# A weight load in two parts, parity copies, and another exit in a depthwise-separable kernel

## Chip, cores, metric

One core of one Trainium2 chip. The metric is the device time of one execution in microseconds (us), the median of several runs. The kernel before took 575.16 us (575.14 to 575.4, 3 runs). The engines are TensorE (PE; its weight loads are PEld), VectorE (DVE), ScalarE (ACT), GpSimd (POOL) and SyncE (SP).

## The reference, cut to what matters

```python
x:  (1, 384, 384, 384) bf16      # 147456 rows of 384 channels, 113 MB
dw: (1, 1, 384)                  # a 1x1 depthwise filter: one factor per channel
pw: (384, 384)
out = einsum('bhwc,cd->bhwd', x * dw, pw)
```

With a 1x1 filter this is one matrix product: x times a 384 x 384 matrix whose row c is dw[c] * pw[c].

## The kernel before

The rows are worked in 288 blocks of 512. VectorE transposes 32 x 32 squares of 32-bit words (channel pairs), so that channel pairs come to lie on the 32 partitions of a square. TensorE then runs 48 matmuls a block, four at a time, each on its own 32 rows of the array. ScalarE moves each finished block out of PSUM, and SyncE stores it.

Since TensorE works on four row groups, each needs its own copy of the scaled weights, split by even and odd channel. That makes six 128 x 768 pieces of `w_r`, made at the start by matmuls with a selector matrix `sel_w` that already holds dw:

```python
nc.scalar.dma_start(dw_row[:], ...).then_inc(s_dw, 16)
load_x(0, nc.scalar)                                           # x0
nc.sync.dma_start(pw_n[:], pw.rearrange("(k p) d -> p k d", p=P)).then_inc(s_pw, 16)
...                                                            # x1, x2, ... on SyncE
idle_work(4)                                # TensorE: 4 rounds of 4 matmuls on ones
nc.tensor.wait_ge(s_dw, 16)
for k in range(3): ...                      # dw onto partitions, by three matmuls
idle_work(4)
nc.tensor.wait_ge(s_pw, 16)
times = {(1, 1): 3, (2, 0): 2}              # some products are repeated
for k in range(3):
    nc.tensor.wait_ge(s_sw, k + 1)          # selector k is ready (VectorE)
    for r in range(2):
        if k == 2:
            nc.tensor.wait_ge(*w_done[r])   # copy r has left PSUM
        for v in [0, 1] * times.get((k, r), 1):
            mm = nc.tensor.matmul(PS[(k + 1) % 2][:, 2 * r + v, :D],
                lhsT=sel_w[64 * v : 64 * v + 64, k, r, :, :]...,
                rhs=pw_n[64 * v : 64 * v + 64, k, :], ..., tile_position=(64 * v, 0))
        mm.then_inc(s_w)                    # then a copy on ScalarE or VectorE into w_r
```

The main loop follows; its first step waits for four of the six copies. At the end:

```python
nc.sync.wait_ge(s_a[je % 2], je // 2 + 2 + k)     # ScalarE's half of the last block
nc.sync.wait_ge(s_d, k + 1)                       # VectorE's half
nc.sync.dma_start(dst[:, part], src[:, part]).then_inc(s_o[g % NR], 16)
```

## Time and profile before

| | kernel before |
|---|---|
| median time | 575.16 us |
| profiled span | 573.2 us |
| first main matmul | 6.90 us |
| block spacing | 1.950 us, all 287 steps |
| last block's copies begin, to the end | 4.47 us |

Shares of busy time say little here: TensorE is busy 99% of the span by design, also with idle matmuls. The useful views are the chain of waits, which says what held the start of the loop, and the timeline of the two ends. The prediction below shows and reads those lines. One line of that timeline: start us, us, engine, line, operation, tiles, count, and the idle time before it with its releaser.

```profile
5.49 0.66 PE L239 MATMUL ps<-pw_n,sel_w 64*128 64x384 bf16 x6 [0.17 <-ACT w_r L289]
```

Six matmuls take 0.66 us, because they run two at a time on the two halves of the array's rows.

### The profile page before, as it was taken

Reading aid. Unit: us, or ns where it says so; the run is one execution under the profiler, and the core shown is the slowest. Engines: PE = TensorE matmul, PEld = TensorE weight load, DVE = VectorE, ACT = ScalarE, POOL = GpSimd, SP = SyncE. Lnnn points to the kernel's source line nnn. Section 1 sums busy time; section 2 is a strip of 40 time slices with the busy share of each in tenths; the row PEclk is TensorE's granted clock in tenths of the full one; section 3 lists DMA queues with packets and bytes.
Section 4 is the critical chain, followed back from the end, with each engine's and each line's share of the span. In section 5 each row is a group of like instructions: output and inputs, shape, how many; then the busy total and the mean of one; then the engine's idle time right before and its main releaser. Section 6 shows DMA issues by size and latency. Waiting matters only on the chain.

```text
span 573.2 us, 29721 instructions
## 1 busy us (share of the span) xinstructions
PE 566.5 (99%) x13877; PEld 417.7 (73%) x13877; DVE 509.0 (89%) x584; ACT 418.7 (73%) x297; POOL 0.5 (0%) x5
## 2 busy tenths in 40 slices
PE   8999999999999999999999999999999999999996
PEld 5777777777777777777777777777777777777774
DVE  7899999999999999999999999999999999999995
ACT  6777777777777777777777777777777777777775
POOL 0000000000000000000000000000000000000000
PEclk9999999999999999999999999999999999999999
DMA  8999999999999999999999999999999999998676
GB/s 361 427 334 432 422 424 433 443 413 424 430 420 411 391 396 433 399 387 401 425 400 389 406 423 400 399 394 423 411 387 428 403 391 406 413 398 365 265 288 238
DMA packets 26452, 226.88 MB, mean 396 GB/s; under 512 B 1225, under 2 KB 6986, under 8 KB 22602
## 3 DMA queue, kind: packets, MB, share of 16 engines
q1 hardware_dynamic: 25264, 225.61, 97.1%
q10 hardware_dynamic: 1178, 1.18, 0.6%
q14 instruction: 9, 0.07, 0.0%
q8 instruction: 1, 0.02, 0.0%
HBM read 113.54 MB, written 113.25 MB: 396 GB/s over the span
## 4 chain that ended last, share of the span: by engine, by line
PE 97%; DMA 1%; ACT 1%; DVE 0%; issue 0%; SPq 0%
PE ps L191 97%; DMA pw_n<-in_pw_dram 1%; DMA out_dram<-O 0%; ACT w_r L289 0%; ACT O L326 0%; DVE O L324 0%; PE ps L239 0%; SPq L359 0%; SPq L102 0%
## 5 line engine op out<-in xcount | busy, mean ns | idle before, releaser
L191 PE MATMUL ps<-w_r,T 32*128 32x384 bf16 x13824 | 561.8, 321 | 0.7 <-ACT w_r L289 0.7
L276 DVE STREAM_TRANSPOSE T<-X 128x384 uint32<-128x384 uint32 x572 | 502.2, 880 | 53.9 <-DMA X<-in_x_dram 0.4
L191 PEld LDWEIGHTS ps<-w_r,T 32*128 32x128 bf16 x13824 | 415.9, 93 | 146.6 <-issue 1.0
L326 ACT CAST O<-ps 128x1536 bf16<-128x1536 f32 x287 | 412.7, 1438 | 147.3 <-PE ps L191 147.3
L289 ACT CAST w_r<-ps 128x768 bf16<-128x768 f32 x5 | 3.6, 820 | 1.0 <-PE ps L239 1.0
L208 PE MATMUL ps<-const-bfloat16-1.0 32*128 32x384 bf16 x32 | 2.9, 515 | 1.1 <-SPq L102 1.1
L276 DVE STREAM_TRANSPOSE T<-Xl 128x384 uint32<-128x384 uint32 x4 | 3.5, 880 | 0.4
L324 DVE CAST O<-ps 128x384 bf16<-128x384 f32 x2 | 1.0, 553 | 3.1 <-DMA out_dram<-O 3.1
L264 ACT ACT_TABLE_LOAD x1 | 1.3, 1283 | 1.9 <-issue 1.9
L208 PEld LDWEIGHTS ps<-const-bfloat16-1.0 32*128 32x128 bf16 x32 | 1.1, 125 | 1.7 <-issue 1.4
L239 PE MATMUL ps<-pw_n,sel_w 64*128 64x384 bf16 x18 | 1.8, 324 | 0.3 <-ACT w_r L289 0.2
L239 PEld LDWEIGHTS ps<-pw_n,sel_w 64*128 64x128 bf16 x18 | 0.7, 94 | 1.8 <-DMA pw_n<-in_pw_dram 0.9
L289 DVE CAST w_r<-ps 128x768 bf16<-128x768 f32 x1 | 1.0, 957 | 0.9 <-PE ps L239 0.9
L294 DVE TENSOR_REDUCE sel<-eye 128x64 f32<-128x128 bf16 x1 | 0.3, 290 | 1.4 <-POOL eye L254 1.4
L323 ACT CAST O<-ps 128x384 bf16<-128x384 f32 x2 | 0.9, 482 | 0.5 <-PE ps L191 0.5
L301 DVE COPY dw_f<-ps 128x3 f32<-128x3 f32 x1 | 0.2, 161 | 1.0 <-PE ps L221 1.0
L304 DVE TENSOR_SCALAR sel_w<-sel,dw_f 128x256 bf16<-128x256 f32 x3 | 0.9, 348 | 0.0
L221 PEld LDWEIGHTS ps<-const-bfloat16-1.0,dw_row 1*128 1x128 bf16 x3 | 0.2, 102 | 0.6 <-DMA dw_row<-in_dw_dram 0.6
L264 ACT COPY warm<-const-float32-0.0 128x1 f32<-128x1 f32 x2 | 0.3, 190 | 0.0
L254 POOL TENSOR_SCALAR_AFFINE_SELECT eye<-const-bfloat16-1.0 128x128 bf16<-128x128 bf16 x1 | 0.3, 292 | 0.6 <-SPq L102 0.6
L221 PE MATMUL ps<-const-bfloat16-1.0,dw_row 1*128 1x1 bf16 x3 | 0.2, 167 | 0.0
L348 POOL MEMSET const-bfloat16-1.0<- 128x1 bf16 x1 | 0.1, 102 | 0.0
(3 smaller groups left out, 0.3 us busy)
## 6 DMA issues: line engine op xcount, KB each, us to landing
X<-in_x_dram SPq DMA_DIRECT2D x26, 3840.0 KB, 21.2
out_dram<-O SPq DMA_DIRECT2D x26, 3840.0 KB, 27.1
X<-in_x_dram SPq DMA_DIRECT2D x3, 1536.0 KB, 17.4
out_dram<-O SPq DMA_DIRECT2D x4, 768.0 KB, 9.2
out_dram<-O SPq DMA_DIRECT2D x2, 1536.0 KB, 14.7
X<-in_x_dram SPq DMA_DIRECT2D x3, 768.0 KB, 7.4
X<-in_x_dram SPq DMA_DIRECT2D x1, 2304.0 KB, 19.1
out_dram<-O SPq DMA_DIRECT2D x1, 2304.0 KB, 10.9
```

What stands on the lines that cost most here:

```text
L191: mm = nc.tensor.matmul(PS[s][:, q, :D], lhsT=Ts[s][32 * q : 32 * q + 32, b, par::2], rhs=w_r[32 * q : 32 * q + 32, b, par, :], start=(b, ...
L208: nc.tensor.matmul(PS[0][:, 2 * (i % 2) + i // 2, :D], lhsT=ones[32 * i : 32 * i + 32, 0:P], rhs=ones[32 * i : 32 * i + 32, :], start=True ...
L221: mm = nc.tensor.matmul(PS[1][:, 0, D + k : D + k + 1], lhsT=dw_row[:, P * k : P * k + P], rhs=ones[0:1, 0:1], start=True, stop=True,)
L239: mm = nc.tensor.matmul(PS[(k + 1) % 2][:, 2 * r + v, :D], lhsT=sel_w[64 * v : 64 * v + 64, k, r, :, :].rearrange("p q w -> p (q w)"), rhs ...
L254: nc.gpsimd.affine_select(out=eye[:], in_=ones[:, 0:P], pattern=[[-1, P]], compare_op=mybir.AluOpType.is_equal, fill=0.0, base=0, channel_ ...
L264: nc.scalar.copy(warm[:, s : s + 1], nc.const_aps.tensor(0.0, [P, 1], F32)).then_inc(s_a[s])
L276: ins = nc.vector.transpose(out=Tw[:, 3 * h : 3 * h + 3], in_=Xw[:, :, j, 96 * h : 96 * h + 96].rearrange("p k (b w) -> p b k w", w=32),)
L289: o = nc.vector.tensor_copy(out, in_) if e == 0 else nc.scalar.copy(out, in_)
L304: nc.vector.tensor_scalar_mul(sel_w[:, k], sel[:].unsqueeze(2).to_broadcast([P, 2, 4, 32]), dw_f[:, k : k + 1]).then_inc(s_sw)
L323: nc.scalar.copy(Ov[:, q, j, :], PS[s][:, q, :D]).then_inc(s_a[s])
L324: nc.vector.tensor_copy(Ov[:, q + 1, j, :], PS[s][:, q + 1, :D]).then_inc(s_d)
L326: a = nc.scalar.copy(Ov[:, :, j, :], PS[s][:, :, :D])
```

## The change

The intent: get the first part of pw sooner and in longer runs, so that the weight copies and the loop start sooner, and shorten the tail. Rows 0 to 255 of pw go two per partition (1536 bytes in one run), then x0, then rows 256 to 383 onto 64 partitions, all on SyncE's queue. Since neighbouring rows now share a partition, the products are split by row parity. The critical section is opened and closed by GpSimd, and SyncE's two last waits change places.

```diff
-    with tc.tile_critical():
+    with tc.tile_critical(sync_engine=mybir.EngineType.Pool, no_gpsimd_drain=True):
...
+                nc.sync.wait_ge(s_d, k + 1)
                 nc.sync.wait_ge(s_a[je % 2], je // 2 + 2 + k)
-                nc.sync.wait_ge(s_d, k + 1)
...
-        load_x(0, nc.scalar)
-        nc.sync.dma_start(pw_n[:], pw.rearrange("(k p) d -> p k d", p=P)).then_inc(s_pw, 16)
+        nc.sync.dma_start(
+            pw_n[:, 0:2].rearrange("p t d -> p (t d)"),
+            pw[0 : 2 * P, :].rearrange("(p t) d -> p (t d)", t=2),
+        ).then_inc(s_pw, 16)
+        load_x(0)
+        nc.sync.dma_start(
+            pw_n[0:64, 2:4].rearrange("p t d -> p (t d)"),
+            pw[2 * P : C, :].rearrange("(p t) d -> p (t d)", t=2),
+        ).then_inc(s_pw2, 16)
...
-        for k in range(3):
+        for k in range(4):
+            c0, m = (k, P) if k < 2 else (2 * P + k - 2, 64)
             mm = nc.tensor.matmul(
-                PS[1][:, 0, D + k : D + k + 1],
-                lhsT=dw_row[:, P * k : P * k + P],
+                PS[1][0:m, 0, D + k : D + k + 1],
+                lhsT=dw_row[:, c0 : c0 + 2 * m - 1 : 2],
...
+                tile_position=(0, 0),
...
                 for v in [0, 1] * times.get((k, r), 1):
+                    row, slot, h = (64 * v, r, k) if k < 2 else (0, 2 + r, v)
...
-                        tile_position=(64 * v, 0),
+                        tile_position=(row, 0),
```

Left out: the waits that go with it, four selectors instead of three, another order of two steps within a block, and the places in `w_r` that the copies write.

More of the change, by code (lines that the diff above doesn't have):

```diff
@@ L67 @@
     psum = ctx.enter_context(tc.tile_pool(name="psum", bufs=1, space=bass.MemoryType.PSUM))
-    pw_n = consts.tile([P, 3, D], BF16, name="pw_n")
+    pw_n = consts.tile([P, 4, D], BF16, name="pw_n")
     eye = consts.tile([P, P], BF16, name="eye")
     sel = consts.tile([P, 2, 32], F32, name="sel")
-    sel_w = consts.tile([P, 3, 2, 4, 32], BF16, name="sel_w")
+    sel_w = consts.tile([P, 4, 2, 4, 32], BF16, name="sel_w")
     w_r = consts.tile([P, NB, 2, D], BF16, name="w_r")
     dw_row = consts.tile([1, C], BF16, name="dw_row")
-    dw_f = consts.tile([P, 3], F32, name="dw_f")
+    dw_f = consts.tile([P, 4], F32, name="dw_f")
     warm = consts.tile([P, 2], F32, name="warm")
@@ L94 @@
     s_pw = nc.alloc_semaphore("s_pw")
+    s_pw2 = nc.alloc_semaphore("s_pw2")
     s_df = nc.alloc_semaphore("s_df")
@@ L178, in w_ps @@
             return PS[0 if i in (2, 3) else 1][:, 2 * (i % 2) : 2 * (i % 2) + 2, :D]
-        steps = [(b, par) for b in range(4) for par in range(2)] + [(4, 0), (5, 0), (4, 1), (5, 1)]
+        steps = [(b, par) for b in (0, 2, 1, 3) for par in range(2)] + [(4, 0), (5, 0), (4, 1), (5, 1)]
         def supertile(s, rv):
@@ L200, in supertile @@
                         mm._wait_ge(s_a[s], rv)
-                    if (b, par) in ((2, 1), (5, 1)) and q == 3:
+                    if (b, par) in ((1, 1), (5, 1)) and q == 3:
                         mm.then_inc(s_pe)
@@ L232 @@
         for k in range(3):
-            nc.tensor.wait_ge(s_sw, k + 1)
             for r in range(2):
+                if k == 0:
+                    nc.tensor.wait_ge(s_sw, r + 1)
                 if k == 2:
+                    if r == 0:
+                        nc.tensor.wait_ge(s_pw2, 16)
+                        nc.tensor.wait_ge(s_sw, 4)
                     nc.tensor.wait_ge(*w_done[r])
                 for v in [0, 1] * times.get((k, r), 1):
+                    row, slot, h = (64 * v, r, k) if k < 2 else (0, 2 + r, v)
                     mm = nc.tensor.matmul(
                         PS[(k + 1) % 2][:, 2 * r + v, :D],
-                        lhsT=sel_w[64 * v : 64 * v + 64, k, r, :, :].rearrange("p q w -> p (q w)"),
-                        rhs=pw_n[64 * v : 64 * v + 64, k, :],
+                        lhsT=sel_w[row : row + 64, slot, h, :, :].rearrange("p q w -> p (q w)"),
+                        rhs=pw_n[row : row + 64, slot, :],
                         start=True,
                         stop=True,
-                        tile_position=(64 * v, 0),
+                        tile_position=(row, 0),
                     )
@@ L287, in w_out @@
             e, k, r = w_eng[i], i // 2, i % 2
-            out, in_ = w_r[:, 2 * k : 2 * k + 2, r, :], w_ps(i)
+            out, in_ = (w_r[:, k : k + 3 : 2, r, :] if k < 2 else w_r[:, 4:6, r, :]), w_ps(i)
             o = nc.vector.tensor_copy(out, in_) if e == 0 else nc.scalar.copy(out, in_)
@@ L295 @@
             out=sel[:],
-            in_=eye[:].rearrange("p (v w r) -> p r w v", v=2, r=2),
+            in_=eye[:].rearrange("p (v h w) -> p h w v", v=2, h=2),
             op=mybir.AluOpType.add,
@@ L300 @@
         nc.vector.wait_ge(s_df, 1)
-        nc.vector.tensor_copy(dw_f[:], PS[1][:, 0, D : D + 3]).then_inc(s_dwf)
-        nc.vector.wait_ge(s_dwf, 2)
-        for k in range(3):
+        for k, m in ((0, P), (2, 64)):
+            nc.vector.tensor_copy(dw_f[0:m, k : k + 2], PS[1][0:m, 0, D + k : D + k + 2]).then_inc(s_dwf)
+        for k in range(4):
+            m = P if k < 2 else 64
+            nc.vector.wait_ge(s_dwf, 2 + k // 2)
             nc.vector.tensor_scalar_mul(
-                sel_w[:, k], sel[:].unsqueeze(2).to_broadcast([P, 2, 4, 32]), dw_f[:, k : k + 1]
+                sel_w[0:m, k], sel[0:m].unsqueeze(2).to_broadcast([m, 2, 4, 32]), dw_f[0:m, k : k + 1]
             ).then_inc(s_sw)
```

## The prediction

> **What bounds the kernel now.** I read the engine shares first, then the costliest groups, then the chain that ended last, then the timeline of the two ends of the run. From the page, parts 1 and 5 (busy us, share, instructions; then busy, mean ns | idle before, releaser):
>
> ```profile
> PE 566.5 (99%) x13877; PEld 417.7 (73%) x13877; DVE 509.0 (89%) x584; ACT 418.7 (73%) x297; POOL 0.5 (0%) x5
> L191 PE MATMUL ps<-w_r,T 32*128 32x384 bf16 x13824 | 561.8, 321 | 0.7 <-ACT w_r L289 0.7
> ```
>
> TensorE is busy for 99% of the span, and its 13824 main matmuls waited once, for 0.7 us, before the first of them. The evictions on ScalarE start every 1.95 us (9.07, 11.03, 12.97, 14.93 in the timeline) from the first block of 512 rows to the last: 288 blocks x 1.95 = 561.6 us. VectorE (89%) and the DMA engines (mean 396 GB/s) run close behind, but never make TensorE wait. Nothing in this stage is changed except the order of two pairs of matmuls inside a block. So the change can only move the two ends, 573.2 - 561.8 = 11.4 us in all, 2.0% of the span. The chain of waits shows both (start us, us, what):
>
> ```profile
> 1.02 3.10 DMA pw_n<-in_pw_dram
> 4.12 0.05 issue
> 4.17 0.36 PE ps L239 x2
> 4.53 0.02 issue
> 4.55 2.21 ACT w_r L289 x3
> 6.76 0.14 issue
> 6.90 557.90 PE ps L191 x13728
> ...
> 566.29 2.52 DMA out_dram<-O
> 568.80 1.01 DVE O L324 x2
> ```
>
> The head: load of pw (lands at 4.12), the first pair of weight matmuls (pw times dw, spread over partitions), three copies of weights on ScalarE, then the main loop at 6.90. The chain names the load as the cause, but the timeline has something beside it (window 3.3 to 4.2, TensorE; then the forms of line 208 and of the weight matmuls, ns min/median/max):
>
> ```profile
> 2.78 1.22 PE L208 MATMUL ps<-const-bfloat16-1.0 32*128 32x384 bf16 x11
> 4.17 0.34 PE L239 MATMUL ps<-pw_n,sel_w 64*128 64x384 bf16 x2 [0.17 <-DMA pw_n<-in_pw_dram]
> ...
> L208 PE MATMUL ps<-const-bfloat16-1.0 x32: 476/522/523, 1.1 to 3.5; 32*128 32x384 bf16 x32
> L239 PE MATMUL ps<-pw_n,sel_w x18: 319/322/333, 4.2 to 5.8; 64*128 64x384 bf16 x18
> ```
>
> TensorE itself was idle only 0.17 us before the first weight matmul: the idle matmuls that keep it busy were recorded until 4.00. Their rounds start 320 ns apart, the weight pairs 162 ns apart: the clock rose between 3.5 and 4.17. The granted clock of the page does not show this early part; the trace's clock record has full clock from 3.91.
>
> The tail (SyncE's queue; then line 102, the closing of the critical section, and one row of the closing barrier):
>
> ```profile
> 569.44 0.82 SPq L142 DMA_DIRECT2D out_dram<-O  x2
> ...
> L102 SPq EVENT_SEMAPHORE  x3: 17/28/28, 572.1 to 572.3; - x3
> L102 SPq NOP  x2: 13/16/18, 0.8 to 572.4; - x2
> ...
> L359 POOLq EVENT_SEMAPHORE  x4: 17/17/17, 572.6 to 573.1; - x4
> ```
>
> The last two stores are issued at 569.44 and 569.90, land by 571.90, and then 1.1 us of semaphores follow.
>
> **What the skill says.** "TensorE: Matmul & The Clock Gate", Part 1 (the HAM clock gate): the array runs at half clock until a window of about 3.4 us has been busy, and the window runs freely, so the moment differs from run to run. The trace agrees in kind: 320 ns against 162 ns a round, busy from 1.12, raised at 3.91. "DMA: Bandwidth & Descriptors", section Issuing engines are not separate DMA queues: SyncE's and ScalarE's transfers share the same 16 engines, so moving x0 from one to the other gives no bandwidth, only an order. The trace shows the mixing: x0 (ScalarE's queue) begins at 3.21 and interleaves with the last pw packets, which end at 3.71. Same page, Queues, rings and completion order: on an engine, descriptors of one ring are taken in order. So in the new kernel x0 cannot delay the first pw load, and the second pw load queues behind x0.
>
> **The change part by part.**
>
> *Entry through GpSimd.* SyncE's NOP at 0.79 released the others at 0.82, and its first DMA went out at 1.02. GpSimd raises the barrier at 0.68 and can release directly after; I put -0.03 us on ScalarE and -0.05 us on SyncE.
>
> *pw in two loads.* Before: 384 packets of 768 B, first packet 2.11, last 3.71, landing 3.55 to 4.12, that is about 0.4 us after the packets. Only 103 GB/s flowed from 2.0 to 2.8 (some early packets took 240 to 520 ns instead of 36), 341 GB/s from 2.8 to 3.3. The first load now has 128 packets of 1536 B, 197 KB instead of 295 KB, 8 per engine. At 36 ns per 768 B that is 8 x 70 = 0.56 us of transfer, after a slow start of some 0.4 us: estimate packets done at 2.05 + 0.4 + 0.56 = 3.0 to 3.2, landing 3.4 to 3.6 against 4.12. The load gains 0.5 to 0.7 us.
>
> *What of this reaches TensorE.* The last idle round starts at 3.42 (one row group, which carries the dw matmuls, at 3.48) and occupies its rows for 320 ns: until 3.74 and 3.80. The fourth dw matmul adds 0.026 us there (their spacing), and the earlier entry takes about as much away. The first two scaled selectors (VectorE, 0.35 us each, 0.27 us apart) are ready at 3.3 and 3.56, also earlier. So the first weight pair starts at about 3.77, bounded by the idle matmuls, not by the load: 0.40 us earlier. It begins in the last 0.1 us of half clock, though (full clock from 3.91): rows stream 0.24 us instead of 0.16. Net gain of the first copy on ScalarE 0.40 - 0.08 = 0.32 us: 4.55 becomes 4.23. The three copies at 0.69 us and their end do not change, so the main loop starts at 6.90 - 0.32 = 6.58.
>
> *Does anything else hold the loop?* x0 follows on SyncE's ring: its 393 KB at 390 GB/s take 1.0 us after the first load, landing near 4.6 (5.60 before). VectorE's weight copy (957 ns) ends near 5.35, its first transpose near 6.2, before the 6.43 at which the third ScalarE copy ends. Second pw load: 98 KB behind x0, landing near 4.9; its matmuls need the first ScalarE copy out of PSUM anyway (5.03). x1 near 5.8, needed at 6.7. The group for block 10 landed at about 24.0; TensorE will want it transposed at 6.58 + 19.5 = 26.1, and two transposes take 1.6 us: it holds, with 0.5 us to spare. The total bytes are the same and the early queue is always fed (0.47 us per issue against 0.25 to 1.0 us of data each).
>
> *Matmul order and row parity.* Same 48 matmuls a block, same waits at the same places. All four first copies are awaited before the first step either way. Zero.
>
> *Last waits in the other order.* At the end VectorE's copy is the later one (569.35 against ScalarE's 569.20; 569.82 against 569.58). Before, a separate wait of SyncE passed at 569.38 and the store only followed at 569.44, 58 ns later. Now the separate wait (ScalarE's copy) passes early and the store itself waits for VectorE. Second store: 569.90 becomes 569.84, -0.055 us.
>
> *Exit through GpSimd.* After its own last wait (572.10) SyncE raised a semaphore, waited for all engines to answer, then closed: 572.10, .20, .28, .35, .41, .48, .55, and GpSimd's barrier at 572.58. In the new program the others pass long before, and SyncE goes from its drain through two waits to the barrier: the steps of 93 and 73 ns fall away. -0.165 us.
>
> Sum: 0.32 + 0.055 + 0.165 = 0.54 us. 575.16 - 0.54 = 574.6.
>
> **The rivals.** (a) *The whole load gain passes*: if TensorE followed the load, the loop would start 0.5 to 0.7 us earlier: about 574.3. The chain of waits speaks for it, the 0.17 us idle row against it. (b) *The small first load is no faster*, because its start is latency: landing at 3.9, gain 0.15 us, sum 0.37: 574.8. The 103 GB/s at the start speaks for it; the fewer bytes per engine against. (c) *The clock rises later*: the window is free, and the weight matmuls or even the first main matmuls run at half clock; an earlier start then gains half or nothing: 574.9 to 575.2. The three times of before (575.14, 575.16, 575.4) are already 0.26 us apart, so some of this is in both kernels. (d) *VectorE or the loads become the bound at block 10*, and the head's gain is given back there: 575.0. The spare time worked out above is thin but positive.
>
> **Range and chances.** The head can give 0.1 to 0.7 us, the tail 0.15 to 0.25, the clock's phase plus or minus 0.25: 574.1 to 575.2. A change of 2% would be 11.5 us, as much as both ends together; nothing of that size is touched. Within 2%: 0.98.
>
> **What would show it.** Right: the main loop's first matmul at 6.5 to 6.65; TensorE idle under 0.1 us before the first weight matmul, whose start is near 3.77 while pw's first load has landed by 3.6; block spacing still 1.95 us; from the issue of the last store to the end of the span 3.1 us, where it is 573.2 - 569.9 = 3.3 us now. Wrong: a wait for the load before the weight matmuls (b), a wait of TensorE for transposes near 26 us (d), weight pairs 320 ns apart (c), or a changed closing sequence longer than 1.1 us.

## The result

The changed kernel took 575.38 us (574.83 to 575.67, 6 runs) against 575.1 (574.89 to 575.4, 6 runs). The ratio is 1.0004, with a 95% interval of 0.9991 to 1.0017: the same within 2%, but above the predicted range of 574.1 to 575.2. Ratios are the mean time of one kernel's fast runs over that of the other's of the same rounds, so not quite the ratio of the medians quoted here.

The interval is three times as wide as the 0.5 us in question, so a single time settles nothing. The argument below rests on where instructions stand in the traces, and on medians as support. The main groups of the changed kernel's page, in the columns of the prediction's first fence:

```profile
PE 568.1 (99%) x13878; PEld 355.1 (62%) x13878; DVE 508.2 (89%) x586; ACT 418.9 (73%) x297; POOL 0.5 (0%) x5
...
L199 PE MATMUL ps<-w_r,T 32*128 32x384 bf16 x13824 | 561.8, 321 | 0.0
```

The main loop is untouched: 561.8 us, and the blocks again stand 1.950 us apart. Its chain of waits:

```profile
1.12 1.46 PE ps L216 x14
2.57 0.22 PE ps L230 x3
2.79 1.40 PE ps L216 x15
4.19 2.03 PE ps L253 x12
6.23 0.01 issue
6.24 1.32 PE ps L253 x6
7.56 557.84 PE ps L199 x13728
...
569.41 0.55 DVE O L340
569.95 0.47 DVEq L103
```

No load stands in the head of the chain any more. It is TensorE from 1.12 us on: idle matmuls (line 216), dw matmuls (230), idle matmuls, weight matmuls (253), loop. The loop's first matmul is at 7.50 us instead of 6.90. (The chain's own entry says 7.56, because it counts the last weight matmul up to its recorded end.) The last six weight matmuls take 1.32 us where the kernel before needed 0.66. All matmuls of the weights together (ns min/median/max, first and last start), with the landings of the two loads in us from their issue:

```profile
L253 PE MATMUL ps<-pw_n,sel_w x18: 322/524/524, 4.1 to 7.2; 64*128 64x384 bf16 x18
...
DMA to landing us min/median/max: 2.4/3.3/4.3
```

A median of 524 ns is half clock, which here lasted until 6.64 us by the trace's clock record, against 3.91 us in the profile before. The first load landed at 3.31 (2.4 after its issue at 0.95), the second at 6.19 (4.3 after 1.87). The three ScalarE copies that the loop waits for take 2.40 us, where the kernel before needed 2.21:

```profile
4.67 2.40 ACT L303 CAST w_r<-ps 128x768 bf16<-128x768 f32 x3 [1.59 <-PE ps L253]
```

Two things can hold the loop's start, and one rule fits all 20 profiles: the first main matmul stands 0.14 us after the end of the third ScalarE copy or 0.26 us after the start of the last weight matmul, whichever is later. In the kernel before it is the copy (6.75 + 0.14). In the changed kernel the copy ended at 7.07 and would have allowed 7.21; the last weight matmul (7.24 + 0.26) holds it until 7.50.

The loads themselves slow down. Three stretches of one us in the changed kernel (stretch, length, busy time and count by engine, granted clock, DMA share, GB/s; the column of the granted clock shows 1.00 and not the half clock of this early part):

```profile
3.00:4.00 1.00, 1.00 (x16) 0.31 (x8) 1.00 (x5) 0.08 (x1) 0.00 (x0) 1.00 0.89 335
4.00:5.00 1.00, 1.00 (x10) 0.43 (x8) 0.17 (x2) 0.33 (x1) 0.00 (x0) 1.00 0.74 124
5.00:6.00 1.00, 1.00 (x8) 0.30 (x4) 1.00 (x2) 1.00 (x2) 0.00 (x0) 1.00 0.95 333
```

The 124 GB/s between 4 and 5 us, at the end of the second line, is the thing to see. The DMA engines were busy 0.74 of that time with few bytes: packets of the second pw load took up to 895 ns, where 65 is usual, and packets of x up to 920, where 121 is usual.

The tail did shrink. The changed kernel's closing lines (SyncE's last stores; then line 103, the close of the critical section):

```profile
569.98 0.85 SPq L143 DMA_DIRECT2D out_dram<-O  x2
...
L103 PEldq DRAIN  x1: 1105/1105/1105, 568.2 to 568.2; - x1
...
L103 SPq DRAIN  x1: 7/7/7, 572.7 to 572.7; - x1
```

TensorE's answer is already under way at 568.2, long before SyncE is done, and SyncE has one drain of 7 ns left. From the start of the last block's copies to the end it is 4.26 us, where it was 4.47. In the trace the last store leaves 27 ns after VectorE's last copy instead of 81.

So 0.21 us won at the end and 0.60 us lost at the start give the 0.4 us by which the two profiled spans differ (573.6 against 573.2).

### The profile page after: what moved, and what is told of

Its sections match the earlier page's. It is cut to its first block, busy times and chain, and to the rows that moved or that the text cites. A ratio compares the mean times of both kernels' runs of the same rounds, so it can differ in the third digit from the quotient of the medians.

```text
span 573.6 us, 29728 instructions
## 1 busy us (share of the span) xinstructions
PE 568.1 (99%) x13878; PEld 355.1 (62%) x13878; DVE 508.2 (89%) x586; ACT 418.9 (73%) x297; POOL 0.5 (0%) x5
## 4 chain that ended last, share of the span: by engine, by line
PE 98%; DMA 0%; ACT 0%; DVE 0%; DVEq 0%; issue 0%
PE ps L199 97%; PE ps L253 1%; PE ps L216 0%; DMA out_dram<-O 0%; ACT O L342 0%; DVE O L340 0%; DVEq L103 0%; PE ps L230 0%
## 5 line engine op out<-in xcount | busy, mean ns | idle before, releaser
L199 PE MATMUL ps<-w_r,T 32*128 32x384 bf16 x13824 | 561.8, 321 | 0.0
L199 PEld LDWEIGHTS ps<-w_r,T 32*128 32x128 bf16 x13824 | 352.6, 93 | 209.1 <-issue 0.3
L253 PE MATMUL ps<-pw_n,sel_w 64*128 64x384 bf16 x18 | 3.4, 467 | 0.0
```

What stands on the lines that cost most here:

```text
L199: mm = nc.tensor.matmul(PS[s][:, q, :D], lhsT=Ts[s][32 * q : 32 * q + 32, b, par::2], rhs=w_r[32 * q : 32 * q + 32, b, par, :], start=(b, ...
L253: mm = nc.tensor.matmul(PS[(k + 1) % 2][:, 2 * r + v, :D], lhsT=sel_w[row : row + 64, slot, h, :, :].rearrange("p q w -> p (q w)"), rhs=pw ...
```

## The experiments

Eighteen runs were made. None was refused, all were correct, and every verdict is "same" within 2%. Each call had the kernel before on the same chip; its medians were 575.03 to 575.07 in all of them. Three runs in all took about 579 us (in after_again, idle3 and tail_only_again, one each). They count as fast by the 1.5% rule and widen those ratios, so medians are quoted. What happens in them was not profiled.

Theory 1 was that the phase of the clock window alone had moved the head; theory 2, that the second load lands late; theory 3, that the new dw matmuls hold TensorE.

**before_again**: no edit.

> The kernel before, unchanged, as a second look at it. Theory 1 (the phase of the clock window alone moved the head): the rise of the clock falls at another place between 3 and 7 us than 3.91, and the main loop then starts later than 6.90 if it falls late, by up to 0.6 us; Theories 2 and 3 (the second pw load lands late; the dw matmuls take longer) say nothing of it. Ratio to the kernel before 1.000, within 0.0004 by noise.

Measured 575.04 (574.8 to 575.15). The clock rose at 6.49 us instead of 3.91, and the loop started at 7.05 instead of 6.90. TensorE, window 2.3 to 4.2:

```profile
2.38 0.53 PE L208 MATMUL ps<-const-bfloat16-1.0 32*128 32x384 bf16 x3
2.44 0.19 PE L221 MATMUL ps<-const-bfloat16-1.0,dw_row 1*128 1x1 bf16 x2
2.50 1.44 PE L208 MATMUL ps<-const-bfloat16-1.0 32*128 32x384 bf16 x13
3.96 0.50 PE L239 MATMUL ps<-pw_n,sel_w 64*128 64x384 bf16 x2
```

The phase is real. The loop came only 0.15 us later, but in this profile pw landed 0.21 us sooner (3.91 against 4.12), and the first pair with it (3.96 against 4.17). Counted from the first pair, the late rise costs 0.36 us (3.09 to the loop instead of 2.73). In the changed kernel this stretch is 3.37, so theory 1 explains a good part of the loss, but not the last 0.28 us. The loads ran at 406 GB/s between 4 and 5 us.

**after_again**: no edit.

> The changed kernel, unchanged, as a second look. Theory 1: the clock rises elsewhere than at 6.64 us and the weight matmuls and the start of the main loop follow it: with an early rise the loop starts near 6.6. Theory 2: the second pw load lands again at 5.5 us or later and the last weight matmuls wait for it, wherever the clock is; loop at 7.0 or later. Theory 3: the first weight pair starts at 4.1 again, wherever the clock is. Ratio 1.0004 expected from the first six runs.

Measured 575.5 (575.0 to 579.12, 6 runs). With the clock up at 6.37 the first weight pair stood at 4.13 again (theory 3), the second load landed at 5.54 (theory 2), and the loop started at 7.27. Of the 0.22 us to before_again, 0.17 are there in the first weight pair already (4.13 against 3.96).

**tail_only**: the kernel before with `tile_critical(sync_engine=Pool, no_gpsimd_drain=True)` and the two last waits swapped; nothing else.

> The kernel before with the exit (and entry) through GpSimd and the other order of the last waits alone; no change to the head. All theories: from the start of ScalarE's last two copies to the end 4.26 us instead of 4.47, so 0.21 us less: ratio 0.9996, about 574.9. If the tail gain isn't real in timed runs: 1.000.

Measured 574.75 (574.64 to 574.92), ratio 0.9995. The stretch from the last copies to the end is 4.257 us, as predicted. The tail's part is worth having.

**pw2_first**: the second load issued before x0.

```diff
-        load_x(0)
         nc.sync.dma_start(pw_n[0:64, 2:4]..., pw[2 * P : C, :]...).then_inc(s_pw2, 16)
+        load_x(0)
```

> The changed kernel with the second pw load issued before x0 instead of behind it. Theory 2: it lands by about 4.0 us instead of 6.2, the last weight matmuls wait for ScalarE's first copy only (about 5.4), the loop starts by 6.6 to 7.2 and the time is 0.3 to 0.5 us under the changed kernel's: ratio 0.9994 to 0.9998. Theories 1 and 3: nothing gained beyond noise, ratio 1.0003.

Measured 575.08 (574.67 to 575.34). The second load landed at 5.02, not at 4.0: the slow stretch came along, with 155 GB/s between 3 and 4 us now and 366 between 4 and 5. The loop started at 7.21. By the medians this is 0.3 to 0.4 us better than the changed kernel, as theory 2 said, though its landing time was wrong. The loop is now held by the third copy (7.07 + 0.14) and no longer by the last product.

**idle3**: one idle round less ahead of the weights.

```diff
         mm.then_inc(s_df)
-        idle_work(4)
+        idle_work(3)
```

> The changed kernel with three rounds of idle matmuls in the second block instead of four. If TensorE's own queue of idle matmuls holds the first weight pair (4.13 in both profiles of the changed kernel, with the load landed by 3.35), the pair moves one half-clock round earlier, to 3.80 (-0.32 us), and the first ScalarE copy from 4.67 to 4.35. If the load or the selectors held it, it stays at 4.1. The clock may rise later for the missing round. Time, if the loop follows: 0.1 to 0.3 us under the changed kernel's, ratio 1.0000 to 1.0003; if the late second load holds the loop, unchanged (1.0005).

Measured 575.56 (574.79 to 579.02, 4 runs). The first pair moved to 3.81, 0.31 us earlier, so TensorE's own queue held it and not the load, as the prediction had said. But the loop started at 7.45: an earlier first pair is worth nothing while the last product holds the loop. The second load came at 5.97. The block after the second also came 0.47 us late, because the third chunk of x landed at 10.75 us.

**dw_wide**: four dw matmuls 128 columns wide, as they were before, not pinned to a tile; the second load's rows lie on partitions 64 to 127 for that.

```diff
-            c0, m = (k, P) if k < 2 else (2 * P + k - 2, 64)
+            c0 = k if k < 2 else P + k - 2
...
-                tile_position=(0, 0),
```

> The changed kernel with all four dw matmuls 128 columns wide and without a tile position, as the three of before were; the rows of the second load sit on partitions 64 to 127 instead of 0 to 63. Theory 3 (the narrow, pinned dw matmuls drain the array between tile shapes): the idle matmuls resume 0.1 us after the first dw matmul instead of 0.35, the last idle round starts at 3.42 to 3.48 instead of 3.67, the first weight pair at 3.87 instead of 4.13, all 0.25 us earlier. Theory 2: the second load still lands at 5.0 or later with packets of over 500 ns. Time 0.1 to 0.25 us under the changed kernel's.

Measured 575.26 (575.01 to 575.49). TensorE in the changed kernel, window 2.3 to 4.2:

```profile
2.38 0.41 PE L230 MATMUL ps<-const-bfloat16-1.0,dw_row 1*128 1x1 bf16 x4
2.73 1.47 PE L216 MATMUL ps<-const-bfloat16-1.0 32*128 32x384 bf16 x16
4.13 0.50 PE L253 MATMUL ps<-pw_n,sel_w 64*128 64x384 bf16 x2
```

and in dw_wide:

```profile
2.37 0.23 PE L230 MATMUL ps<-const-bfloat16-1.0,dw_row 1*128 1x1 bf16 x2
2.45 0.51 PE L216 MATMUL ps<-const-bfloat16-1.0 32*128 32x384 bf16 x3
2.47 0.19 PE L230 MATMUL ps<-const-bfloat16-1.0,dw_row 1*128 1x1 bf16 x2
2.52 1.44 PE L216 MATMUL ps<-const-bfloat16-1.0 32*128 32x384 bf16 x13
3.89 0.82 PE L252 MATMUL ps<-pw_n,sel_w 64*128 64x384 bf16 x4
```

The idle matmuls resume beside the dw matmuls again, and the first pair comes at 3.89 instead of 4.13: theory 3's step is shown. The Trainium skill offers a reason in "TensorEngine Tiling (Array Packing)", Key Properties: changing the tiling mode drains TensorE. A 64-column matmul among 128-column ones may be such a change; the starts in the changed kernel's trace are 57 ns apart between two wide dw matmuls, 91 from wide to narrow, and 120 from narrow to the next idle matmul. How much of it is the width and how much the pinned position was not told apart. A pause that fits the same property stands in every kernel with the idle queue as bound: from the last idle round's start plus its 320 ns to the first weight pair (32-row to 64-row tiles) pass 0.135 us (dw_wide: 3.439 + 0.320 to 3.894). The time hardly moved: the second load landed at 6.27, the loop started at 7.40, and the block after the second came 0.19 us late, behind a chunk of x that landed at 10.41.

**dw_wide_full**: the second load fills all 128 partitions (rows 128 to 383).

```diff
-            pw_n[64:P, 2:4]..., pw[2 * P : C, :]...     # as in dw_wide
+            pw_n[:, 2:4]...,    pw[P : C, :]...
```

> As dw_wide, and the second pw load fills all 128 partitions (rows 128 to 383, half of it never used, 98 KB more). Theory 2a (the 64-partition load is what goes slowly): its packets take 65 ns, no stretch under 300 GB/s between 4 and 5 us, landing by 4.9 in spite of twice the bytes, SyncE's issues back at 0.43 us; loop start 0.1 to 0.4 us earlier than in dw_wide. Theory 2b (any second small load of pw rows goes slowly): packets of 500 to 900 ns again, landing 5.5 or later. Time at or below the tail alone (574.75) for 2a.

Measured 575.35 (575.34 to 575.35), landing at 6.03. SyncE's issue of this load took 424 ns instead of 552, but the slow stretch stayed. The count of partitions is not its cause (theory 2b).

**wide_full_act**: the same load on ScalarE's queue.

```diff
-        load_x(0)
-        nc.sync.dma_start(
+        nc.scalar.dma_start(
             pw_n[:, 2:4]..., pw[P : C, :]...).then_inc(s_pw2, 16)
+        load_x(0)
```

> As dw_wide_full, with the second load issued on ScalarE's queue behind dw_row instead of on SyncE's behind x0. It starts about 1 us earlier and interleaves with x0. If only its place in the ring made it late: landing by 4.3, x0 by 4.9. If its packets are slow by themselves: as in dw_wide_full. The loop is then bound by the third ScalarE copy, 6.5 (clock up by 4) to 6.9 (clock up after 6); time 574.5 to 574.8.

Measured 574.74 (574.59 to 574.92). The load still landed at 5.96, so its place in the ring did not cure it. The clock rose early here (4.86), and the loop started at 7.08. This comes to the same time as the tail alone.

Theory 4 asked whether having everything early on SyncE's ring makes the loads slow (4a), or the extra small load (4b).

**tail_x0sp**: tail_only with x0 moved to SyncE behind the single pw load.

```diff
-        load_x(0, nc.scalar)
         nc.sync.dma_start(pw_n[:], ...).then_inc(s_pw, 16)
+        load_x(0)
```

> The kernel before with the tail of the change (as tail_only, 574.75) and one part of the head: x0 on SyncE's queue behind the single pw load, nothing on ScalarE's queue but dw_row and the two late blocks. Theory 4a (with everything early on one ring the stream stalls: landings of x1, x2 and of the group for block 10 come 1 to 2 us late, as in all five kernels with x0 or the second pw load rearranged): x1 lands at 7.0 or later instead of 6.06, x2 past 9.3, the group of block 10 at 24.6 or later. Theory 4b (the extra small load does it): landings as in tail_only, x1 by 6.2, block 10's group by 23.9. Time: 574.75 in 4b; up to 575.0 in 4a.

Measured 574.83 (574.7 to 575.65). From 4 to 6 us the loads ran at 307 to 310 GB/s (tail_only: 384 and 427), x1 landed at 6.68 (between the 6.2 of 4b and the 7.0 of 4a) and block 10's group at 24.45. Over these 2 us the rate is 309 GB/s, against 406 in tail_only and 236 in after_again. That is about half of the effect without any second load: a part of 4a.

**x0_act**: the changed kernel with x0 back on ScalarE's queue.

```diff
         nc.scalar.dma_start(dw_row[:], ...).then_inc(s_dw, 16)
+        load_x(0, nc.scalar)
         nc.sync.dma_start(pw_n[:, 0:2]..., ...).then_inc(s_pw, 16)
-        load_x(0)
         nc.sync.dma_start(pw_n[0:64, 2:4]..., ...).then_inc(s_pw2, 16)
```

> The changed kernel with x0 back on ScalarE's queue: both pw loads on SyncE, one behind the other. Theory 4a: no hole; second pw load by 4.2, x1 by 6.2, block 10's group by 23.9, loop start 6.7 to 7.2 by the clock, time 574.8 to 575.0. Theory 4b: second pw load past 5.0 and x1 past 7.0, as in the changed kernel; 575.3. The first weight pair stays at 4.13 in both (dw matmuls unchanged).

Measured 575.03 (574.85 to 575.27). From 4 to 6 us 272 and 298 GB/s, x1 at 7.90, second load at 5.39: part of 4b as well. Neither half of the theory holds alone.

**wide_x0_act** and **wide_x0_act_again**: the edits of x0_act and of dw_wide together.

> As x0_act, with the wide dw matmuls of dw_wide as well: two pw loads on SyncE, x0 on ScalarE, dw matmuls without a tile switch. If both losses of the head are named rightly, first weight pair at 3.89 and no hole: loop start 6.5 to 6.95 by the clock, time 574.5 to 574.7, under the tail alone (574.75) by 0.1 to 0.2 us; if the hole stays, 575.1 to 575.3.

> The same as wide_x0_act once more: first weight pair at 3.89 whatever the clock does; time 574.5 to 574.8. At 575.0 or more the first result (574.66) was luck of the clock.

Measured 574.66 (574.43 to 575.05) and, on another chip, 575.02 (574.79 to 575.2). In the second profile dw itself landed at 2.80 instead of 2.2, so that even the first pair stood at 4.34: against the expectation, it follows dw too. The first result was partly luck.

**wide_pw2_first**: the edits of dw_wide and of pw2_first together; x0 stays on SyncE.

> The changed kernel with the wide dw matmuls and the second pw load ahead of x0 on SyncE (x0 stays on SyncE). If the two named causes account for the loss of the head: first weight pair 3.89, second load by 5.1, loop start 6.5 to 7.0 by the clock, time 574.6 to 574.8, as wide_x0_act. If x0 on SyncE costs by itself (it lands at 5.8 in pw2_first, so the first transpose waits for it): loop start up to 7.0, time 574.8 to 575.0.

Measured 574.95 (574.78 to 575.18). The first pair stood at 3.89, the second load landed at 4.64, and yet the loop started at 7.38. Two named causes were gone and the loss was still there.

**runs768**: the changed kernel's two loads cut into 768-byte runs by padding the tile's rows (the runs then cannot merge).

```diff
-    pw_n = consts.tile([P, 4, D], BF16, name="pw_n")
+    pw_n = consts.tile([P, 4, D + 16], BF16, name="pw_n")
...
-            pw_n[:, 0:2].rearrange("p t d -> p (t d)"), ...
+            pw_n[:, 0:2, :D], ...
```

> The changed kernel with the same two loads in runs of 768 bytes (the tile's rows are padded so that neighbours don't merge): 256 and 128 packets of 36 ns instead of 128 and 64 of 65. If the 1536-byte runs have to do with the slow stretch: no packets over 500 ns after 4 us, second load by 5.0, x1 by 6.3, time 575.0. If not: as the changed kernel, 575.3 to 575.5, second load past 5.3. The first load lands later than at 3.35 either way, by up to 0.3 us.

Measured 575.54 (575.24 to 576.44), second load at 5.92, 221 GB/s between 4 and 5 us. The run length is not the cause of the slow stretch; the long runs bring the first load in sooner (3.35 to 3.31 against 3.78).

**wide_x0_idle3**: the edits of wide_x0_act and of idle3 together.

> As wide_x0_act with one idle round less. The pair would be free at 3.57, so it is then held by the first load (3.35) and the selectors (3.35 and 3.6): first weight pair at 3.5 to 3.65 instead of 3.89, loop 0.2 to 0.3 us earlier if the second load (5.15) is in time, 574.4; a later rise of the clock could take that back.

Measured 574.99 (574.77 to 575.38). The first pair came at 3.57, but the loop started at 7.28. Its chain of waits has all of the time on TensorE:

```profile
3.64 3.71 PE ps L252 x18
7.35 557.84 PE ps L199 x13728
```

Eighteen weight matmuls back to back, 3.7 us. The second load had landed at 5.11, and the third copy ended at 6.51, which would have allowed a start at 6.65. In the trace the last six start at 5.47, 5.79, 6.11, 6.43, 6.75 and 7.03, one at a time. In before_again they start in three pairs. This is the third cause, and neither the prediction nor the first theories had it. In the changed kernel both halves of the last product contract the same 64 rows of pw, on the same rows of the array, and they do not run side by side. Six matmuls in a row take 6 x 0.32 = 1.92 us at half clock or 6 x 0.163 = 0.98 at full clock, against half of that in pairs. The page named above says it from the other side: different tiles work in parallel.

**after_once**: the changed kernel without the repetition in that product.

```diff
-        times = {(1, 1): 3, (2, 0): 2}
+        times = {(1, 1): 3}
```

> The changed kernel with the repetition of the first half of the last weight product taken out (times without (2, 0): four matmuls in a row instead of six; the result is the same). If TensorE's row of serial matmuls holds the loop, the loop starts 0.3 us (full clock) to 0.64 us (half clock) earlier than the row of six would let it, but not before the third ScalarE copy plus 0.14 (7.21): 575.1 to 575.3 instead of 575.4 to 575.5. If only the landing of the second load held it: unchanged.

Measured 575.0 (574.73 to 575.11), against 575.38 and 575.5 for the changed kernel. Its chain:

```profile
4.19 2.93 PE ps L253 x16
7.13 0.09 issue
7.21 557.90 PE ps L199 x13728
```

The loop now starts at 7.21, which is 0.14 us after the third ScalarE copy (7.07), though the clock rose at 6.61 and the second load landed at 5.78. So the row of serial matmuls no longer holds the loop. As an estimate from this trace, two more matmuls at 0.163 us would have put the last one at 7.13 and the loop at 7.39: the repetition is worth 0.17 us here. The time moved more than these profiles' loop starts (7.50 and 7.27 before, 7.21 now) account for; the second load's landing differs from run to run.

**wide_x0_idle3_once**: an edit against each of the three causes (x0 on ScalarE, so that the second load does not stand behind it; wide dw matmuls; no repetition), and one idle round less.

```diff
+        load_x(0, nc.scalar)                  # ahead of both pw loads, as in x0_act
...
-            c0, m = (k, P) if k < 2 else (2 * P + k - 2, 64)
+            c0 = k if k < 2 else P + k - 2    # and no tile_position, as in dw_wide
...
-        idle_work(4)
+        idle_work(3)
...
-        times = {(1, 1): 3, (2, 0): 2}
+        times = {(1, 1): 3}
```

> wide_x0_idle3 with the repetition taken out. In its profile the six serial matmuls ended at about 7.2 while the third ScalarE copy was done at 6.51. If they hold the loop: start at 6.65 to 6.85 instead of 7.28, time 574.5 to 574.7 instead of 574.99. If not: 575.0.

Measured 574.6 (574.27 to 574.8), against 575.07 (574.82 to 575.8, 11 runs) for the kernel before on the same chip, ratio 0.9991 with an interval of 0.9978 to 1.0004. Its chain:

```profile
3.64 2.97 PE ps L252 x16
6.61 0.04 issue
6.66 557.96 PE ps L199 x13728
```

The loop starts at 6.66, the earliest of all profiles, 0.14 us after the third copy (6.51, as in wide_x0_idle3). Not all of the 0.63 us to wide_x0_idle3 is the repetition: the clock rose at 6.05 here and at 6.97 there. Two more matmuls at 0.163 us would have put this loop at 6.87 (an estimate as above), so 0.21 us are the repetition's. The slow stretch is still there (255 GB/s from 4 to 6 us, second load at 5.54); it only holds nothing any more. All five runs lie under all eleven of the kernel before, though the interval includes 1. It has the lowest median found. Whether the other repetition, (1, 1), is worth keeping was not tried.

**tail_only_again**: no edit to tail_only.

> Tail alone once more, beside the other two on the same chip: 574.75 within 0.1, 0.3 us under the kernel before; loop start 6.9 to 7.05.

Measured 574.91 (574.65 to 579.09, 6 runs), of which the profiled run was one of the longer ones (575.91). Its dw arrived at 3.12 us, the first pair stood at 4.63, the clock rose at 8.49, and the loop started at 7.72. The tail was 4.25 us all the same. So a 768-byte load that landed 0.89 us later than in tail_only, with a late clock, cost this head 0.79 us in one run (7.72 against 6.93), more than the change could win; 0.60 of it is there in the first pair (4.63 against 4.04).

## Why the prediction was wrong

What was right:

- *What bounds the kernel, and what the loop does.* Block spacing stayed at 1.950 us, and the order of steps cost nothing.
- *The tail.* 0.055 + 0.165 = 0.22 us were predicted; 0.21 was measured in the profile (4.47 to 4.26; 3.14 us from the last store's issue to the end, where 3.1 was forecast), and tail_only lies 0.29 and 0.16 us under the kernel before by its two medians.
- *The first load.* Predicted to land at 3.4 to 3.6, it landed at 3.31 and 3.35 (4.12 before). *What of this reaches TensorE*: that the idle matmuls and not the load hold the first pair was right, and idle3 showed it.
- *The entry*: SyncE's first issue went from 1.02 to 0.95, a little more than the 0.05 us predicted.

What was wrong is the head. The loop started 0.92 us after the forecast 6.58: the first pair came 0.36 us later than forecast, the stretch from there to the end of the third copy was 0.28 longer, and the last product held the loop for another 0.28. By the prediction's steps:

1. "The fourth dw matmul adds 0.026 us": it added 0.25 (from the first dw matmul to the last idle round, against before_again). For a wide one the figure was right: 0.028 in dw_wide. The narrow, pinned matmuls stop the idle matmuls from running beside them (2.73 instead of 2.38). Together with a 0.135 us pause before the weight pair that the step had left out, the first pair stood at 4.13 instead of 3.77. dw_wide gave 0.24 of it back. The selectors, forecast for 3.3 and 3.56, came at 3.38 and 3.64, still early enough.
2. "The three copies at 0.69 us and their end do not change", and the net 0.32 us built on it: the rise of the clock at 3.91 was taken from one profile as if it were fixed. It lay between 3.91 and 8.49 us in the 20 profiles, and 19 of them were later than 3.91. At half clock the products ahead of the third copy take longer than the copies, so the third copy ends 2.4 us after the first begins (changed kernel, and before_again too) instead of 2.2, and the first copy begins 0.16 us later after its pair: 0.36 together, of which the sum had only 0.08. Rival (c) had named this, but the central estimate did not use it.
3. "Second pw load ... landing near 4.9; its matmuls need the first ScalarE copy out of PSUM anyway", and "the early queue is always fed": it landed at 6.19 and 5.54, because the loads fell to 124 and 167 GB/s between 4 and 5 us. x1, forecast near 5.8, landed at 8.03 and 7.64. In pw2_first and wide_pw2_first, where the second load went ahead of x0, the slow stretch lay between 3 and 4 us instead (155 and 203 GB/s).
4. Left out altogether: the last product's matmuls became serial, 1.32 us for what took 0.66 in the profile before and 0.97 in before_again, with its late clock. The diff shows it (`row` is 0 for both halves where it was `64 * v`). That this row held the loop is read in the trace of wide_x0_idle3, and after_once and wide_x0_idle3_once show that it does not once the repetition is gone. In the changed kernel's first profile steps 3 and 4 hold the loop together; in after_again, where the load was in time, the row alone cost 0.05 us.

Rival (a), the whole load gain, fell: the load is out of the chain and nothing came of it. Rival (b) fell: the load was faster. Rival (c) happened, in both kernels. Rival (d) did not: block 10's group landed at 24.55 and no block was late there. A milder form of it came at another place in dw_wide and idle3, where the block after the second waited for x.

Open: what makes packets take 500 to 900 ns in the slow stretch. The number of partitions (dw_wide_full), the length of runs (runs768) and the ring (wide_full_act, x0_act) do not explain it alone. It follows the second load when that is moved, and half of it is there with x0 alone moved (tail_x0sp). Open too is what the 579 us runs are, and how much the clock's phase and the landings, which no run could set, had in each difference of medians.

## What to carry to other kernels

When a load is brought forward, list what else the waiting engine still has in its own queue, and whether the new form of the work still runs side by side: operands folded onto fewer partitions can turn paired matmuls into serial ones. One profile of a start-up is one throw of the clock's phase, so take two before a number like "full clock from 3.91" goes into a sum. A part that shortens the very end, like the swapped waits, is kept in full whatever happens before it (4.25 to 4.27 us from the last copies to the end in all 18 profiles that have it).

## What the Trainium skill lacked or had wrong

- "TensorE: Matmul & The Clock Gate", Part 1 (the HAM clock gate): it gives a transition around 4 us into activity, varying by about 500 ns from run to run. With TensorE busy from 1.12 us on, the rise here lay between 3.91 and 8.49 us in 20 profiles: 2.79 us into activity in the kernel before, less than a window, and 5.52 in the changed kernel, whose TensorE shows no gap. That the window runs freely agrees: the rise and the fall at the end are 570.03 us apart in the kernel before and 566.61 in the changed one, and these differ by one window, 3.41.
- "TensorEngine Tiling (Array Packing)", Key Properties: that a mode change drains the array is there, without a cost. Here it was 0.135 us from 32-row to 64-row tiles at half clock, and some 0.25 us with two 64-column matmuls and a pinned position in between 128-column ones. That a drain is the cause is argued from the page, not shown.
- "DMA: Bandwidth & Descriptors": no section has the slow stretch found here, in which packets of 1536 bytes took up to 895 ns and the 16 engines together fell to 124 GB/s for one us near the start of a kernel.
- No page says how the closing of a critical section differs by the engine that closes it: from the last store's landing to the end 1.15 us with GpSimd and `no_gpsimd_drain=True`, 1.33 with SyncE, 0.17 us less. The two settings were not told apart.
